# Written-out engine orders, FFN blocks placed among attention, paired output projections: an adaLN block on one Trainium2 core

## The chip, the cores and the metric

The kernel runs on one core of a Trainium2 chip. The metric is the device time of one execution in microseconds; several runs of each kernel are taken, beside runs of the kernel before on the same chip. The profiled run gives a span (first to last instruction), which lies about 2 us under the time of the same run (227.9 under 230.01 before, 216.1 under 217.79 after). Engines: PE is TensorE (PEld its weight loads), DVE VectorE, ACT ScalarE, POOL GpSimd. TensorE writes its results to the banks of a memory called PSUM. The names of these results in the profiles: ps_w warm-up, ps_c and ps_m the six vectors made from c, ps_t a norm's transposes, ps_qk, ps_v, ps_l logits, ps_o values, ps_ot transposes of o, ps_g gates, ps_wo output projection, ps_h and ps_y the two halves of the FFN.

On one core a run is called slow when it is over 1.5% above the fastest of the same kernel. Where I compare kernels I use fast runs, and say so where a trace is of a slow one.

## The reference, cut to what matters

```python
x = A_x                                              # 2048 x 448, bf16
sa, ca, ga, sb, cb, gb = (silu(c) @ w_mod)           # six vectors of 448
h = layernorm(x) * (1 + ca) + sa
x = x + ga * (local_attention(h @ wqkv) @ wo)        # 16 heads of 28; 8 keys per query, every second row
h = layernorm(x) * (1 + cb) + sb
x = x + gb * (silu(h @ w1) @ w2)                     # the FFN, 448 -> 1792 -> 448
```

Rows are split by parity (`par`), so that "every second row" is a run of neighbours. Attention works on 18 blocks: nine of 114 queries (`e0` to `e8` in the new code) for each parity. A block is two groups of logits on TensorE, two exponentials on ScalarE, a mask on VectorE, a values product, a division, a transposition. FFN and both norms work in four chunks of 512 rows.

## The kernel before: the parts that the change touches

The kernel lists about 700 operations with dependencies, durations and buffers, and lets a small scheduler put them into an order. The engines then take their instructions strictly in that order.

```python
class Plan:
    def emit(self, seed, spread, rounds):          # 12 rounds of list scheduling
        ...
        for _ in range(rounds):
            span, new = self.order(prio)
            if span < self.span:
                self.span, got = span, new
            prio = {i: -t + spread * (rnd.random() - 0.5) for i, t in self.late(new or got).items()}
        ...
```

A number of matmuls without use warm TensorE's clock up at the start:

```python
    def warm_up(o):
        ...
        T.matmul(warm[0][:, 0, :], lhsT=ident[:], rhs=ident[:].unsqueeze(1).to_broadcast([128, 4, 128]), start=True, stop=True)
```

The output projection takes one unit (128 rows of one parity) at a time. D is 448, so the last of the four contraction steps has 64 rows:

```python
    def out_proj(k, i, par):
        def wo_mm(o):
            box["ps"] = onet("ps_wo")                          # one of 2 single PSUM banks
            for kk in range(KT):
                T.matmul(box["ps"][:, 0:D], lhsT=oT[rows_of(kk), kk, par, s0:s0 + 128], rhs=wo[rows_of(kk), kk, :], ...)
```

Logits, QK, V, a norm's transposes and FFN1 use three pairs of banks (`big`); values, transposes of o, gates and FFN2 two single ones (`one`). At the end of the program all exponentials are queued ahead of all silus (cut):

```python
    for k in range(NC):
        first = silus.get(k - LA - 1, [sc_op]) + (exps[k - 1][-1:] if k else [])     # LA = 3, NC = 4
        for b in BLOCKS[k]: ... logits(...); values(...)
        if k >= LA: ffn1(k - LA, exps[k])
    for k in range(NC - LA, NC):
        ffn1(k, silus[k - 1]); ffn2(k - 1)
    ffn2(NC - 1)
```

## Time and profile before

| | before |
|---|---|
| time, median of 3 runs | 228.67 us (227.53 to 229.92) |
| span of the profiled run | 227.9 us (its own time was 230.01) |
| TensorE / VectorE / ScalarE busy | 210.9 / 111.6 / 102.9 us |
| TensorE at half clock, by the record | 11.3 to 14.7, 35.15 to 48.8, 103.4 to 120.5 |
| first V matmul; last matmul | 16.0; 222.5 |
| TensorE idle between these two | 9.1 us |

To read it: TensorE is busy 93% of the span, but a busy TensorE at half clock does half the work. So three things are to be had: the time until the projections can start, idle TensorE after that, and half clock after that. The lines behind the table stand in the prediction.

### The profile page before, as it was taken

How to read it: one execution, taken by the hardware profiler on the slowest of the kernel's cores; microseconds unless marked ns; L12 is line 12 of the kernel's file. 1: busy time of each engine (PE TensorE's matmuls, PEld its weight loads, DVE VectorE, ACT ScalarE, POOL GpSimd, SP SyncE). 2: the span in 40 equal slices, each digit the busy share in tenths (PEclk: the TensorE clock that was granted, in tenths of full speed). 3: DMA queues.
4: the chain of work that ended last, by engine and by line, in shares of the span. 5: the costliest groups of instructions: out<-in, count | busy, mean ns of one | idle time of the engine just before them, and what ended most of it. 6: DMA issues, size and time to landing. Idle time of an engine off the chain costs nothing.

```text
span 227.9 us, 3929 instructions
## 1 busy us (share of the span) xinstructions
PE 210.9 (93%) x1656; PEld 99.3 (44%) x1656; DVE 111.6 (49%) x245; ACT 102.9 (45%) x125; POOL 20.2 (9%) x60
## 2 busy tenths in 40 slices
PE   7899997999899999955999899999999999999990
PEld 2643445434444544434544343435444345444450
DVE  3539795691588485798652735664111021102211
ACT  1118766735786785790667253361215503350000
POOL 6303311000002000150000010111000000000000
PEclk9979995579999999995559999999999999999998
DMA  6999900000000000000000000000000001001111
GB/s 225 347 389 334 305 6 1 0 3 0 3 1 3 0 3 0 3 0 0 4 0 3 0 0 3 0 0 0 23 30 30 0 23 40 20 1 42 43 43 47
DMA packets 7856, 11.28 MB, mean 49 GB/s; under 512 B 536, under 2 KB 6616, under 8 KB 7832
## 3 DMA queue, kind: packets, MB, share of 16 engines
q1 hardware_dynamic: 7824, 10.95, 14.5%
q8 instruction: 15, 0.25, 0.5%
q14 instruction: 9, 0.07, 0.1%
q10 hardware_dynamic: 8, 0.00, 0.0%
HBM read 9.12 MB, written 1.84 MB: 48 GB/s over the span
## 4 chain that ended last, share of the span: by engine, by line
PE 80%; DVE 9%; ACT 4%; issue 2%; DMA 1%; ACTq 0%; DVEq 0%
PE ps_y L705 19%; PE ps_h L681 17%; PE ps_qk L513 10%; PE ps_v L536 6%; PE ps_wo L659 5%; PE ps_t L424 4%; PE ps_l L566 3%; PE ps_h L683 3%; PE ps_o L623 3%; PE ps_m L375 3%; PE ps_t L426 2%; ACT p L574 2%; PE ps_ot L636 2%; DVE st L409 2%; ACT h L433 2%
## 5 line engine op out<-in xcount | busy, mean ns | idle before, releaser
L687 ACT ACTIVATE both<-ps_h 128x1024 bf16<-128x1024 f32 x28 | 28.5, 1024 | 47.6 <-PE ps_y L705 21.6
L705 PE MATMUL ps_y<-w,both 128*128 128x448 bf16 x224 | 44.4, 353 | 0.7 <-DVE ot L710 0.7
L681 PE MATMUL ps_h<-h,w 128*128 128x512 bf16 x168 | 41.8, 389 | 0.0
L574 ACT ACTIVATE p<-ps_l 128x912 bf16<-128x912 f32 (+1 forms) x36 | 31.6, 939 | 11.3 <-PE ps_l L566 11.2
L710 DVE TENSOR_TENSOR ot<-ps_y,x_all 128x448 bf16<-128x448 f32 x16 | 9.7, 622 | 54.2 <-PE ps_y L705 54.2
L705 PEld LDWEIGHTS <-both 128*128 128x128 bf16 x224 | 21.4, 98 | 21.7 <-issue 2.1
L513 PE MATMUL ps_qk<-h,wp 128*128 128x512 bf16 (+1 forms) x128 | 28.9, 399 | 0.0
L681 PEld LDWEIGHTS <-w 128*128 128x128 bf16 x168 | 15.2, 99 | 19.8 <-issue 4.6
L433 ACT ACTIVATE h<-ps_t,modc 128x512 bf16<-128x512 bf16 x18 | 13.0, 776 | 18.3 <-DVE h L435 13.3
L409 DVE BATCH_NORM_STATS2 st<-x_all 128x6 f32<-128x448 bf16 x32 | 19.7, 615 | 3.2 <-DMA x_all<-in_A_x_dram 2.8
L596 DVE TENSOR_TENSOR p<-p,maskb 128x1824 bf16<-128x1824 bf16 (+1 forms) x18 | 19.3, 1094 | 2.4 <-ACT p L574 2.4
L517 ACT CAST qk<-ps_qk 128x1024 bf16<-128x1024 f32 x14 | 14.2, 1013 | 11.6 <-PE ps_qk L513 11.6
L413 POOL TENSOR_TENSOR rs<-mv,epsb 128x2 f32<-128x2 f32 x16 | 4.8, 300 | 133.3 <-DVE mv L410 133.3
L659 PE MATMUL ps_wo<-wo,oT 128*128 128x448 bf16 x64 | 16.4, 356 | 0.0
L513 PEld LDWEIGHTS <-wp 128*128 128x128 bf16 (+1 forms) x128 | 9.3, 98 | 15.7 <-issue 8.1
L536 PE MATMUL ps_v<-wqkv,h 128*128 128x448 bf16 (+1 forms) x72 | 15.9, 379 | 0.1
L566 PE MATMUL ps_l<-qk 28*128 28x114 bf16 (+1 forms) x288 | 13.4, 229 | 2.7 <-ACT p L574 1.7
L662 DVE TENSOR_TENSOR x_all<-ps_wo,x_all 128x448 bf16<-128x448 f32 x16 | 9.9, 617 | 11.0 <-PE ps_wo L659 10.9
L418 DVE TENSOR_SCALAR xn<-x_all,mv,rs 128x448 bf16<-128x448 bf16 x32 | 11.4, 389 | 5.2 <-POOL rs L414 3.5
L424 PE MATMUL ps_t<-ident,xn 128*128 128x128 bf16 x96 | 12.7, 252 | 0.1
L414 POOL TENSOR_TENSOR rs<-rs,negh 128x2 f32<-128x2 f32 x16 | 12.0, 751 | 1.3
L566 PEld LDWEIGHTS <-qk 28*128 28x128 bf16 x288 | 8.2, 101 | 8.1 <-issue 6.4
(77 smaller groups left out, 172.4 us busy)
## 6 DMA issues: line engine op xcount, KB each, us to landing
x_all<-in_A_x_dram SPq DMA_DIRECT2D x4, 448.0 KB, 5.2
out_dram<-ot SPq DMA_DIRECT2D x16, 112.0 KB, 1.7
w<-in_B_w_dram SPq DMA_DIRECT2D x1, 1568.0 KB
both<-in_w_mod_dram SPq DMA_DIRECT2D x1, 1344.0 KB, 11.2
w<-in_B_w_dram SPq DMA_DIRECT2D x1, 1344.0 KB, 14.4
wqkv<-in_A_wqkv_dram SPq DMA_DIRECT2D x1, 1008.0 KB, 7.2
both<-in_w_mod_dram SPq DMA_DIRECT2D x1, 672.0 KB, 5.2
wo<-in_A_wo_dram SPq DMA_DIRECT2D x1, 336.0 KB, 11.1
```

Of the source, the lines that this page charges most:

```text
L409: V.bn_stats(out=st[:], in_=x_all[:, us[j], :])
L424: T.transpose(box["ps"][:, k, 128 * j:128 * j + 128], box[j][:, 128 * k:128 * k + 128], ident[:])
L433: S.activation(out=out_, in_=in_, func=ACTF.Identity, scale=scale, bias=shift)
L513: T.matmul(ps[:, j, :], lhsT=w.rearrange("p h d -> p (h d)"), rhs=h[rows_of(kk, j), kk, :, 128:128 + CP], start=start, stop=stop)
L536: T.matmul(ps[:, par, 0:D], lhsT=h[rows_of(kk, par), kk, par, b0:b0 + 128], rhs=w, start=(kk == 0), stop=(kk == KT - 1))
L566: T.matmul(ps[:, j, g * nq:(g + 1) * nq], lhsT=key, rhs=q, start=True, stop=True)
L574: S.activation(out=out_, in_=ps[:, :, 0:4 * nq].rearrange("p j (g q) -> p j g q", q=nq), func=ACTF.Exp, scale=SCALE)
L596: V.tensor_tensor(out=p, in0=p, in1=maskb[:, 1 if b == 0 else 0, 0:nq].unsqueeze(1).to_broadcast([128, H, nq]), op=ALU.mult)
L659: T.matmul(box["ps"][:, 0:D], lhsT=oT[rows_of(kk), kk, par, s0:s0 + 128], rhs=wo[rows_of(kk), kk, :], start=(kk == 0), stop=(kk == KT - 1))
L681: T.matmul(ps[:, j, :], lhsT=w1[:, kk, c0:c0 + 128], rhs=h[:, kk, :], start=start, stop=stop)
L687: return [(("act", act_ns(1024)), lambda o, ps: S.activation(out=hid[:, k % 2, :, i, :], in_=ps[:], func=ACTF.Silu), after + f2_read.get(k ...
L705: T.matmul(box["ps"][:, 0:D], lhsT=hid[:, k % 2, f % 2, f // 2, 128 * j:128 * j + 128], rhs=w2[:, f // 2 + 7 * (f % 2), :], start=(f == 0) ...
```

## The change

Its intent: replace 12 rounds of scheduling in the program by an order found offline, by a search that models TensorE's clock; let FFN blocks alternate with attention; use the array's two halves in the output projection; let the first norm's four units go one by one. For the projection, the last 64 rows of wo are loaded twice, into both halves (cut below). The diff, cut to its core:

```diff
-WARM = 26
-LA = 3
-SEED, SPREAD, ROUNDS = 0, 2000.0, 12
+WARM, WARM_AT = 22, 1500.0
+SEQ = "e0 e1 e2 e3 e4 s0 e5 e6 s1 e7 e8 s2 s3"
+ORDER = (
+    "42 0 3 2 1 22 23 4 24 25 66 26 32 5 79 40 43 41 30 36 31 44 37 76 34 45 38 80 ..."   # 707 entries, cut
+)
...
+    S.preload_act_table(ACTF.Silu)
+    V.memset(junk[:], 0.0)
     V.memset(c4[:], 0.0)
...
-        T.matmul(warm[0][:, 0, :], lhsT=ident[:], rhs=ident[:].unsqueeze(1).to_broadcast([128, 4, 128]), start=True, stop=True)
+        T.matmul(warm[0][:, 0, :], lhsT=junk[:, 0:128], rhs=junk[:], start=True, stop=True)
...
-            for j in (0, 2):                                  # norm: rstd for two units at once
+            for j in range(0, 4, n):                          # n = 1 for the first norm, else 2
...
-            box["ps"] = onet("ps_wo")
-            for kk in range(KT):
-                T.matmul(box["ps"][:, 0:D], lhsT=oT[rows_of(kk), kk, par, s0:s0 + 128], rhs=wo[rows_of(kk), kk, :], ...)
+            ps = box["ps"] = bigt("ps_wo")
+            for kk in range(KT):
+                for par in range(2):
+                    T.matmul(ps[:, par, 0:D], lhsT=oT[rows_of(kk, par), kk, par, s0:s0 + 128], rhs=wo[rows_of(kk, par), kk, :], ...)
...
+    for kind, n in ((x[0], int(x[1:])) for x in SEQ.split()):
+        if kind == "e": ...                                   # attention block n
+        else:
+            ffn1(n, e_last + s_last, l_last)
+            s_last, f_last = silus[n], f1_read[n]
+            ffn2(n)
...
-    P.emit(SEED, SPREAD, 1 if safe else ROUNDS)
+    P.emit("" if safe else ORDER)
```

## The prediction

> **What bounds the kernel now.** I read the page first, then the windows, then the chain of work that ended last, then TensorE's waits. The page:
>
> ```profile
> span 227.9 us, 3929 instructions
> PE 210.9 (93%) x1656; PEld 99.3 (44%) x1656; DVE 111.6 (49%) x245; ACT 102.9 (45%) x125; POOL 20.2 (9%) x60
> ...
> PE   7899997999899999955999899999999999999990
> ...
> DVE  3539795691588485798652735664111021102211
> ACT  1118766735786785790667253361215503350000
> ...
> PEclk9979995579999999995559999999999999999998
> ```
>
> TensorE (PE) is busy 93% of the span, no other engine half of it. So TensorE's time is the bound, but not all of that time is work: the clock row has two holes, slices 7 and 8 and again 20 to 22, in which the same matmuls take up to twice as long. And VectorE and ScalarE are busy in the first 23 slices, almost free in the last 17: attention stands first, the feed-forward part (FFN) last. Windows cut at a step of 3.413 us show the holes' edges exactly (columns: window, its length, busy times, PEclk):
>
> ```profile
> 31.74:35.15 3.41, 3.41 (x47) 2.17 (x45) 3.38 (x9) 2.75 (x3) 0.78 (x2) 1.00 0.02 5
> 35.15:38.56 3.41, 2.42 (x44) 2.09 (x45) 1.48 (x6) 1.26 (x2) 0.11 (x1) 0.50 0.01 2
> ...
> 100.00:103.42 3.42, 0.47 (x14) 0.27 (x10) 3.39 (x6) 2.50 (x4) 2.40 (x2) 1.00 0.00 0
> 103.42:106.83 3.41, 1.88 (x31) 1.33 (x32) 2.98 (x9) 0.00 (x0) 0.00 (x0) 0.50 0.00 0
> ```
>
> The clock is half in 11.3 to 14.7, 35.15 to 48.8 and 103.4 to 120.5: 34 us. In the window before each fall the array streamed little: the 40 one-column matmuls of ps_m, or an idle PE. The last fall has this wait ahead of it:
>
> ```profile
> PE ps_ot L636 <- DVE o L630: 4.4, 1, 4.4
> PE ps_l L566 <- ACT p L574: 1.7, 4, 1.0
> ```
>
> Between 16.0 (first V matmul) and 130 PE is busy 105.54 of 114.00 us, idle 8.5; from 130 to 222.3 it is idle 0.7, at full clock. The tail from the last matmul to the end is 5.6 us. So what can be won lies before 130: idle time, half clock, and the start.
>
> **The Trainium skill.** "TensorE: Matmul & The Clock Gate", What's actually happening, says that a monitor sets the clock to half or full by how busy the array was in a free-running window of 3413 ns. The trace agrees: all six edges lie on one grid of 3.413 us (35.15 to 48.8 is 4 steps, 103.4 to 120.5 is 5). It gives no threshold. I took one from this trace: columns streamed in a window, at the granted clock, over what the array could stream. The windows that ended in a fall held 0.13, 0.34 and 0.02; the poorest warm ones that did not, 0.42 and 0.44. Cold windows at 0.75 and below stayed cold; those that ended in a rise held 0.82 and more. "TensorEngine Tiling (Array Packing)", Key Properties, says that changing the tiling mode drains TensorE. The trace shows this at the 64-row step of each projection group: weight loads wait 0.37 and 0.20 us for "issue" around it. "ScalarE: Activation LUTs", What ACT_TABLE_LOAD costs, gives about 1283 ns and a drain of 1380 ns; here the load is 1283 ns, and the exponential that follows starts 0.02 us after it, so I use 1.28.
>
> **The work on TensorE.** From the chain, where pieces follow each other without a wait at full clock:
>
> ```profile
> 63.23 1.93 PE ps_wo L659 x8
> 65.16 0.31 PE ps_l L566 x8
> 65.47 1.54 PE ps_v L536 x8
> 67.00 0.31 PE ps_l L566 x8
> ...
> 68.85 0.49 PE ps_o L623 x16
> ...
> 211.75 10.39 PE ps_y L705 x54
> ```
>
> Read so: ps_y 0.192 us a matmul; V 1.53 a block; logits 0.31 a group; values 0.50; in the same way ps_h 3.13 for 16, QK 3.25 for 16, a norm's transposes 0.45 a unit, ps_ot 0.43, ps_g 0.97, ps_m 2.86. The list: ps_y 224 x 0.192 = 43.0, ps_h 43.8, QK 26.0, V 9 x 1.53 = 13.8, output projection 16 x 0.965 = 15.4, transposes 32 x 0.45 = 14.4, logits 36 x 0.31 = 11.2, values 9.0, ps_ot 7.7, ps_m 5.7, gates 1.9. Without the warm-up and what lies before 16.0 (one ps_m, four transposes) 187.4 us is left. Measured from 16.0 to 222.3: 206.3. The excess of 18.9 is 9.1 idle, some 8 to 9 of half clock, and 1.5 to 2 at the boundaries between kinds.
>
> **The change, part by part.**
> *Output projection in pairs.* Sixteen groups of four matmuls become eight groups of eight, in which the two 64-row steps lie on the two halves of the array, as V has them. From 1.93 to 1.53 for two units: 0.4 x 8 = 3.2 us of TensorE time. The trace has PE as the chain there, so I count it whole. Work after the start: 184.2.
> *Order: FFN into attention.* The order of the instructions shows two of the four FFN blocks within attention. Before, at the last pair of logits groups, PE's list had 90 us behind it and DVE's 84, by durations of the trace: the two engines were bound together, and each waited for the other. After, it is 129 against 94. From the ninth pair on (PE's list at about 66 us) every stretch between two pairs has more PE work than ACT or DVE work. I cut PE's new list into pieces of 3.413 us and took their activity: from 70 us on none is under 0.69, so no fall there. The hole at 103 to 120 and its 5 us wait should go: about 9 us. The wait at 126 to 129 too (1.5 us).
> *Table loads.* Exponential and silu alternate: seven loads in place of three, 4 x 1.28 = 5.1 us on ACT, which goes from 103 to 108 of some 216. Off the path, except where PE waits for a fresh table with all three PSUM pairs full.
> *The start.* The silu table is loaded ahead of everything, but on the queue that also issues the load of c (at 1.02 before). That issue moves to about 2.3, c lands near 6.0 in place of 4.74, and sc follows at once: before, sc began at 6.11. Nothing won there. The warm-up no longer needs the identity (1.43 to about 1.1), but has 6 matmuls ahead of c in place of 11, then a gap of over 2 us and 8 more, perhaps cold, which hold ps_m back. The four transposes follow ps_m at once instead of five warm-up matmuls (1.7 us). I take V's start at 15.0 (13.5 to 16.5) for 16.0.
> *First norm.* Four single rstd steps for two double ones: xn was done at 9.3 and the transposes began at 12.25, so it was not on the path; 0 us.
> *Not won: 15 to 45 us.* PE's new order has seven logits groups in a row there. Their seven exponentials take 7 x 0.94 = 6.6 us, the PE work is 2.2 us, and three PSUM pairs let PE run only three ahead: about 3 us idle. My walk through the lists puts the end of these groups at 41.6, before it was 40.4; the new order has one V block more behind it by then. So the first 40 us win nothing but what the start wins. In that idle window the activity is near 0.15, so the clock falls, and comes back in the QK matmuls after it: 2.5 to 3 us. The second ps_m stands among QK matmuls (piece at 0.26, fall if the grid lies badly): 1.2 us on average.
>
> The sum: start 15.0 + work 184.2 + boundaries 1.7 + tail 5.6 = 206.5; losses 3 (first exponentials) + 2.8 (cold after them) + 1.2 (ps_m) + 1.5 (DVE-tied stretch 45 to 70, still as much DVE as PE work) + 0.7 (the two waits for ps_y's banks at the end, which stay) = 9.2. Span 215.7. The time before lies 0.8 over its span: 216.5.
>
> **Rivals.** (1) DVE stays the bound of attention: its work, 111.6 us, is unchanged. For it: to the eighth pair the lists are level, 59.8 PE to 56.5 DVE. Against: FFN blocks lie between after that. If right, 4 to 6 us of idle and one more cold hole: 222 to 224. (2) The waits turn into PSUM waits: the pairs of the projection now take from the three pairs of banks that logits, QK and FFN1 use. For it: FFN1 and QK want two of three at once. Against: two banks of the other kind are freed. If right, 2 to 3 us: 219. (3) The search's order is nearly free of waits on the chip as well: losses of 4 only, 211.
>
> **Range and chances.** The low end is rival 3, 211; the high end rival 1 with a poor start, 222. Within 2% would need over 224, which leaves less than half of the 12 us of idle, cold and pairing won. Faster by over 2%: 0.92; within 2%: 0.07; slower: 0.01.
>
> **What would show it.** Mean clock rising from 0.92 to 0.95 or more with no half-clock window after 70 us, but one near 38 to 45; eight ps_wo runs of 1.53; seven table loads; the first V matmul near 15; PE's last matmul 5.6 us before the end; PE idle from the first V to that under 7 us. It is wrong if the clock falls again after 70 us, if PE waits longest for DVE o or x_all in the middle, or if the first V starts after 17.

## The result, and the profile after

The changed kernel took 217.87 us (median of 4 runs, 216.87 to 219.79), the kernel before 229.09 us beside it. The ratio of the fast runs is 0.953 (95% interval 0.944 to 0.961). Ratios are the mean time of one kernel's fast runs over that of the other's of the same rounds, so not quite the ratio of the medians. The predicted 216.5 us (211 to 222) holds, and the span, 216.1, lies 0.4 from the predicted 215.7. The next lines show that this is partly luck.

The page of the changed kernel, its total line of busy times and three rows of slices:

```profile
PE 201.6 (93%) x1652; PEld 96.3 (45%) x1652; DVE 111.8 (52%) x246; ACT 107.3 (50%) x127; POOL 21.6 (10%) x65
...
DVE  3608934798679886255361620898518441102220
ACT  2006538784487487744755966860453243550000
...
PEclk9999999988999999999999999999999999999998
```

The long hole of the middle is gone: past slice 10 the clock row has no dip. From 130 us to the last matmul VectorE is now busy 33.4 of 80.4 us and ScalarE 31.7; before it was 24.2 and 27.3 of 92.3. The waits of TensorE after the first V (engine, line, what it waited for: us in total, times, longest):

```profile
PE ps_l L569 <- ACT p L577: 1.2, 3, 0.4
PE ps_o L626 <- DVE p L599: 1.1, 1, 1.1
PE ps_l L569 <- DVE h L438: 0.9, 1, 0.9
PE ps_f L774 <- DVE cnt L772: 0.8, 1, 0.8
PE ps_wo L663 <- ACT p L577: 0.3, 1, 0.3
```

The 4.4 us wait for o has no successor. The first three lie between 41 and 47, where the predicted wait for the first exponentials is. Only 1.2 of their 3.2 us end on an exponential; the other 2.0 end on VectorE, which does 2.2 us of gate products for w2 at 43.64 to 45.86 and the mask after them. With these waits comes the one half-clock window that the record shows (window, length, busy times, clock):

```profile
43.34:46.76 3.42, 1.33 (x32) 0.67 (x25) 3.42 (x7) 3.42 (x5) 0.00 (x0) 1.00 0.00 0
46.76:50.17 3.41, 3.23 (x24) 1.29 (x26) 3.38 (x8) 1.12 (x2) 0.00 (x0) 0.50 0.00 0
50.17:53.58 3.41, 3.41 (x35) 1.65 (x32) 3.29 (x5) 2.18 (x3) 0.00 (x0) 1.00 0.02 5
```

TensorE is busy 1.33 of 3.42 us, the clock falls, and 10 QK matmuls take 3.15 us instead of the 2.03 that follow from 3.25 for 16: a loss of 1.1 us.

**What the record hides: the start.** The timeline of PE in the changed kernel (start, duration, ...; what ended the idle time before, in brackets):

```profile
1.26 2.74 PE L349 MATMUL ps_w<-junk 128*128 128x512 bf16 x6 [1.26 <-DVE scT L270]
6.99 0.18 PE L361 MATMUL ps_c<-ident,sc 4*128 4x4 bf16 x1 [2.99 <-ACT sc L356]
7.10 3.60 PE L349 MATMUL ps_w<-junk 128*128 128x512 bf16 x8
10.49 3.36 PE L378 MATMUL ps_m<-scT,both 128*128 128x1 bf16 x40
...
16.50 3.56 PE L349 MATMUL ps_w<-junk 128*128 128x512 bf16 x9
```

Eight warm-up matmuls in 3.6 us are 0.43 us each, twice the 0.217 from start to start of the last two of the nine below. So the clock is at half, although PEclk reads 9 there: in all fourteen traces the record opens with a fall and shows full clock before it, and here the first recorded fall is at 46.8. The durations give the true state. Of the nine warm-up matmuls that begin at 16.50 some seven are slow and the last ones fast: the clock rose at about 19.5. That is on the same grid of 3.413 us as 46.76, 8 steps earlier. The first V matmul runs at 19.90; I had predicted 15.0, and the kernel before had it at 16.0.

So the 11.8 us by which the span fell are made of five terms (both traces are of fast runs, that of the kernel before the slower end of them: 230.01 us beside a median of 228.67):

| term, us | before | after | difference |
|---|---|---|---|
| start to first V | 16.0 | 19.9 | +3.9 |
| work after it (list of the prediction) | 187.4 | 184.2 | -3.2 |
| idle after it | 9.1 | 4.6 | -4.5 |
| half clock and boundaries after it (what is left over) | 10.0 | 1.7 | -8.3 |
| last matmul to end | 5.4 | 5.7 | +0.3 |

### The profile page after: what moved, and what is told of

Read it like the earlier page. It is cut to its first block, busy times and chain, and to the rows that moved or that the text cites. A ratio compares the mean times of both kernels' runs of the same rounds, so it can differ in the third digit from the quotient of the medians.

```text
span 216.1 us, 3926 instructions
## 1 busy us (share of the span) xinstructions
PE 201.6 (93%) x1652; PEld 96.3 (45%) x1652; DVE 111.8 (52%) x246; ACT 107.3 (50%) x127; POOL 21.6 (10%) x65
## 4 chain that ended last, share of the span: by engine, by line
PE 88%; DVE 4%; ACT 2%; DMA 2%; issue 1%; ACTq 0%
PE ps_y L711 20%; PE ps_h L687 18%; PE ps_qk L516 13%; PE ps_v L539 6%; PE ps_wo L663 5%; PE ps_t L427 4%; PE ps_o L626 4%; PE ps_h L689 4%; PE ps_l L569 3%; PE ps_w L349 3%; PE ps_m L378 3%; PE ps_t L429 3%; DMA c<-in_c_dram 2%; PE ps_ot L639 1%; PE ps_ot L641 1%; DVE w L739 1%
## 5 line engine op out<-in xcount | busy, mean ns | idle before, releaser
L711 PE MATMUL ps_y<-w,both 128*128 128x448 bf16 x224 | 45.8, 353 | 0.0
L687 PE MATMUL ps_h<-h,w 128*128 128x512 bf16 x168 | 40.8, 380 | 0.0
L520 ACT CAST qk<-ps_qk 128x1024 bf16<-128x1024 f32 x14 | 14.1, 1013 | 16.5 <-PE ps_qk L516 16.5
L416 POOL TENSOR_TENSOR rs<-mv,epsb 128x2 f32<-128x2 f32 (+1 forms) x18 | 6.1, 337 | 151.2 <-DVE mv L413 151.2
L412 DVE BATCH_NORM_STATS2 st<-x_all 128x6 f32<-128x448 bf16 x32 | 19.5, 609 | 2.6 <-DMA x_all<-in_A_x_dram 2.4
L599 DVE TENSOR_TENSOR p<-p,maskb 128x1824 bf16<-128x1824 bf16 (+1 forms) x18 | 19.5, 1094 | 2.4 <-ACT p L577 2.3
L436 ACT ACTIVATE h<-ps_t,modc 128x512 bf16<-128x512 bf16 x14 | 10.1, 774 | 20.7 <-DVE h L438 18.4
L438 DVE TENSOR_SCALAR h<-ps_t,modc 128x512 bf16<-128x512 bf16 x18 | 8.9, 539 | 13.9 <-ACT h L436 8.3
L539 PE MATMUL ps_v<-wqkv,h 128*128 128x448 bf16 (+1 forms) x72 | 14.3, 355 | 0.0
L569 PE MATMUL ps_l<-qk 28*128 28x114 bf16 (+1 forms) x288 | 11.7, 210 | 2.3 <-ACT p L577 1.2
L663 PE MATMUL ps_wo<-wo,oT 128*128 128x448 bf16 (+1 forms) x64 | 12.8, 354 | 0.3 <-ACT p L577 0.3
L417 POOL TENSOR_TENSOR rs<-rs,negh 128x2 f32<-128x2 f32 (+1 forms) x18 | 12.1, 670 | 1.4
L631 DVE RECIPROCAL rc<-ps_o 114x16 f32<-114x16 f32 (+1 forms) x18 | 4.5, 252 | 14.4 <-PE ps_o L626 14.2
```

Of the source, the lines that this page charges most:

```text
L412: V.bn_stats(out=st[:], in_=x_all[:, us[j], :])
L417: G.tensor_tensor(out=rs[:, j:j + n], in0=rs[:, j:j + n], in1=negh[:, 0:n], op=ALU.pow)
L520: return [(either(act_ns(1024), dve_ns(1024)), lambda o, ps: copy_on(o)(out=qk[:, :, g, :, s0:s0 + CP], in_=ps[:].rearrange("p j (t s) -> ...
L539: T.matmul(ps[:, par, 0:D], lhsT=h[rows_of(kk, par), kk, par, b0:b0 + 128], rhs=w, start=(kk == 0), stop=(kk == KT - 1))
L569: T.matmul(ps[:, j, g * nq:(g + 1) * nq], lhsT=key, rhs=q, start=True, stop=True)
L599: V.tensor_tensor(out=p, in0=p, in1=maskb[:, 1 if b == 0 else 0, 0:nq].unsqueeze(1).to_broadcast([128, H, nq]), op=ALU.mult)
```

## The experiments

My theories were these. A: the pairing saves drains on the path; the start is late because the warm-up stops too early; the alternation fills the waits. B: what pays in the order is that its search knew the clock. C, against B: what pays is a long search, and an order without waits has full windows anyway. D, after the first results: alternation and search are both needed.

All twelve runs gave correct results. "After start" is the time from the first V or QK matmul to the last matmul; idle is TensorE's within it; half clock is what the record shows within it. These four come from the one trace of each run. The medians are of all runs; where some were slow, the fast ones stand beside them.

| run | median us (range of the fast runs) | start | after start | idle | half clock |
|---|---|---|---|---|---|
| before | 228.67 | 16.0 | 206.5 | 9.1 | 30.7 |
| changed kernel | 217.87 (216.9 to 219.8) | 19.9 | 190.5 | 4.6 | 3.4 |
| the same once more | 215.80 (214.8 to 216.9) | 17.9 | 190.5 | 4.6 | 3.4 |
| pairing undone | 219.26 (218.3 to 220.2) | 17.7 | 194.3 | 4.2 | 6.8 |
| 13 warm-ups ahead of c | 217.48 (fast: 213.5, 214.3) | 15.2 | 190.6 | 4.6 | 3.4 |
| 10 ahead, table load later | 215.21 (fast: 213.9 to 216.0) | 16.0 | 190.3 | 4.6 | 3.4 |
| short search, alternating | 225.60 (fast: 220.9) | 14.6 | 204.9 | 5.8 | 37 (slow run) |
| short search, attention first | 227.64 (227.4 to 228.5) | 14.8 | 207.1 | 9.9 | 33 |
| long blind search, alternating | 213.36 (212.6 to 213.9) | 15.7 | 189.9 | 1.9 | 11 |
| long search with clock, alternating | 217.29 (215.4 to 218.0) | 16.0 | 195.0 | 4.4 | 12 |
| long blind search, attention first | 218.84 (217.9 to 220.6) | 15.3 | 195.9 | 3.5 | 20 |
| long blind search, warm-ups moved | 212.89 (211.9 to 213.4) | 16.8 | 188.7 | 1.8 | 10 |

### Pairing undone

```diff
-            for kk in range(KT):
-                for par in range(2):
-                    T.matmul(ps[:, par, 0:D], lhsT=oT[rows_of(kk, par), ...], rhs=wo[rows_of(kk, par), kk, :], ...)
+            for par in range(2):
+                for kk in range(KT):
+                    T.matmul(ps[:, par, 0:D], lhsT=oT[rows_of(kk), ...], rhs=wo[rows_of(kk), kk, :], ...)
```

> The changed kernel with the output projection issued as before: inside each of the eight operations the two units follow each other, four matmuls each, both 64-row steps on the same half. Same order of everything else. Theory A (pairing saves drains on a chain that TensorE bounds): eight ps_wo groups of about 1.93 us in place of 1.43 to 1.59, so +2.5 to +3.2 us, a span near 219. Rival (the saved time falls into waits): less than +1 us.

The chain of the changed kernel, then that of this run, at the same two groups:

```profile
63.08 1.59 PE ps_wo L663 x8
73.18 1.44 PE ps_wo L663 x8
```

```profile
61.93 1.99 PE ps_wo L663 x8
72.43 1.84 PE ps_wo L663 x8
```

It is 0.40 us a group, 0.39 in the median of the seven groups in the chains, so 3.1 us of TensorE's work for eight: the predicted 3.2. But the eighth group (at 162 to 164) gains nothing on the path: the wait for cnt, the program's check of its sums, follows it, and is 0.8 us in the changed kernel and 0.4 here:

```profile
PE ps_f L774 <- DVE cnt L772: 0.4, 1, 0.4
```

So the path gains 2.7 us. The part after the start grew by 3.8 us; the 1.1 left over may go with a second half-clock window that this trace has. Nor is all of the 0.39 a drain (TensorE running empty at a change between full height and 64 rows). By the single records of the trace, a matmul of 448 columns follows the one before it by 0.189 us, the change to 64 rows takes 0.285 and the change back 0.292. The pair saves one such turn of 0.19, since the two 64-row matmuls start within 3 ns of each other, and 0.20 for one change there and back. The median rose by only 1.4 us against the first runs of the changed kernel and by 3.5 against the second, which shows how much the start blurs: the start in this trace is 17.7 where that of the changed kernel was 19.9, with nothing changed there. Theory A holds for the pairing in the trace, with half of the saving from drains; the rival (under +1 us) falls.

### The start

Thirteen warm-up matmuls ahead of ps_c (entries 48 to 54 of the order moved ahead of 67):

```diff
-    "... 39 67 29 48 81 7 28 49 82 68 50 51 77 52 83 78 53 54 86 55 69 70 ..."
+    "... 39 48 49 50 51 52 53 54 67 29 81 7 28 82 68 77 83 78 86 55 69 70 ..."
```

> The changed kernel with seven of the warm-up matmuls moved from behind ps_c to ahead of it: 13 before c and 1 after, in place of 6 and 8; same 23 in all. Theory A (the 6 matmuls leave a 3 us gap, no window of 3.4 us is full enough, and the clock stays half until 19.5): the warm-up runs without a gap to about 6.8, the clock rises by 8, ps_m starts near 7.5 in place of 10.7, the first V near 14 to 16.5 in place of 19.9, so -3.5 to -5.5 us. Rival (the start is set by the arrival of c and of the weights, the clock is incidental): V within 1 us of 19.9, time the same.

The timeline of PE in this run:

```profile
1.26 4.61 PE L348 MATMUL ps_w<-junk 128*128 128x512 bf16 x13 [1.26 <-DVE scT L269]
6.28 0.17 PE L360 MATMUL ps_c<-ident,sc 4*128 4x4 bf16 x1 [0.41 <-POOL v L337]
6.38 0.39 PE L348 MATMUL ps_w<-junk 128*128 128x512 bf16 x1
6.70 0.21 PE L377 MATMUL ps_m<-scT,both 128*128 128x1 bf16 x3
```

Thirteen in 4.61 us: the first ones slow, the rest fast, so the clock rose before 6. ps_m begins at 6.70 instead of 10.49, the first V at 15.2 instead of 19.9, and the part after it takes 190.6 us, as before. In the trace theory A is right to its number, against the first trace of the changed kernel. Against its second trace (below, first V at 17.9) the gain is 2.7 us, and this run does not tell the clock from the place: there the eight warm-up matmuls between ps_c and ps_m take 3.4 us, and would take 1.7 at full clock; here a single one stands between. In the times it is only half right: two runs at 213.5 and 214.3, two slow ones at 220.7 and 220.9, with a recorded mean clock of 0.936 against 0.975 and more.

> A second look at the version with 13 warm-up matmuls ahead of c. Its four runs were 213.5, 214.3, 220.7 and 220.9. As above: near 213 with some 7 us at half clock, near 220 if the trace shows another long half-clock stretch, and then the place of it.

214.88 us: start 16.2, half clock at 8.3 to 15.1 and for 6.8 us at 42 to 49. What the slow runs do stays open.

Next, the table load moved behind the issue of c, with ten warm-ups ahead:

```diff
-    S.preload_act_table(ACTF.Silu)
...
-    ld_c.append(P.op(("none", 3200.0), none))
+    ld_c.append(P.op(("none", 3200.0), lambda o: S.preload_act_table(ACTF.Silu)))
```

> As the run before it, but the silu table is loaded after the issue of c's load instead of ahead of it, and 10 warm-up matmuls stand before ps_c, 4 after. Theory A: c lands near 4.8 in place of 6.55, sc begins near 4.9; ps_m is then held by the modulation weights, which land near 6.5 to 7, so it starts near 7; the first V another 0.5 us earlier than with 13 matmuls alone, if the clock rises as early. -4 to -6 us against the changed kernel. Rival (table load and issue order do not matter): the same as with 13 matmuls alone.

> A second look at the version with the table load behind the issue of c and 10 warm-up matmuls ahead of it. If the spread of its four runs (213.9 to 220.9) comes from where the clock's windows fall, this trace shows other edges than the first (fall at 8.6, rise at 15, one more stretch at 42 to 45.6), and the time goes with the length of the half-clock stretches: near 213 with 10 us of them, near 220 with 25.

Here the rival wins. The issue of c stands at 1.29 with the load ahead of it or behind it, and sc began at 5.89 and 6.54 in the two looks, against 6.62 and 5.82 in the two of the changed kernel. My sentence "that issue moves to about 2.3" was wrong: the table load runs from 0.81 to 2.09 in the changed kernel, and the issue behind it goes out at 1.29 all the same. c simply lands later here than in the kernel before (4.69 us after its second issue in the first trace, against 3.18), while 0.3 us later in issue; I have not found out why. The two looks took 214.4 and 215.2 us with the first V at 16.0 and 17.8; the spread between them lies in the start, as expected, but neither look was a 220. (The first trace's edges, by its record, are 8.2, 15.1, 42.4 and 45.8; the expectation has them up to 0.4 off.)

The changed kernel once more:

> The changed kernel once more, beside the two searched orders on the same chip. Expected by every theory: 216 to 220 us. Theory A of the start: if the clock rises before 19 us in this trace, because the windows lie otherwise, the first V comes earlier than 19.9 by about that much.

First V at 17.9, 2.0 us earlier than in the first trace, and the same 190.5 us after it, to 0.1. The span is 1.6 us shorter. So in these two traces of one order the part after the start repeats, and the start is what varies. The PE timeline shows how:

```profile
6.30 3.60 PE L349 MATMUL ps_w<-junk 128*128 128x512 bf16 x8
9.69 2.96 PE L378 MATMUL ps_m<-scT,both 128*128 128x1 bf16 x40
12.58 0.34 PE L427 MATMUL ps_t<-ident,xn 128*128 128x128 bf16 x3
14.61 3.47 PE L349 MATMUL ps_w<-junk 128*128 128x512 bf16 x9
17.91 2.27 PE L539 MATMUL ps_v<-wqkv,h 128*128 128x448 bf16 x11
```

Here the same eight warm-up matmuls did raise the clock: ps_m takes 2.96 us instead of 3.36, three transposes 0.34 instead of 0.50. The grid of this trace has an edge at 10.56 (the recorded fall at 44.69 less 10 steps), just behind them; in the first trace an edge at 9.23 cut them in two. After ps_m the clock fell again (13.97 to 17.38 by the record), so the nine warm-up matmuls ahead of V are slow here too. The run with the pairing undone, which has the same start, shows the same with V at 17.7.

### What in the order pays

The changed kernel's operations, ordered by the old scheduler (12 rounds), first alternating, then with attention ahead of FFN:

```diff
-ORDER = ( ... )
+SEED, SPREAD, ROUNDS = 0, 2000.0, 12            # late() and emit() of the kernel before put back
```

```diff
-SEQ = "e0 e1 e2 e3 e4 s0 e5 e6 s1 e7 e8 s2 s3"
+SEQ = "e0 e1 e2 e3 e4 e5 e6 e7 e8 s0 s1 s2 s3"
```

> The changed kernel without its written order: the old scheduler of the kernel before (12 rounds of random priorities, no clock model) orders the same operations, FFN blocks still alternating with attention. Theory A (letting FFN into attention is what fills the waits): no half-clock window after 70 us, TensorE idle between 70 us and its end under 3 us; 215 to 220 us. Rival (the long offline search is what pays): 222 us or more, with new waits for ACT or DVE in the middle.

> As the run with the old scheduler on the changed kernel's operations, but all of attention ahead of all FFN blocks, as in the kernel before. Theory A (the alternation fills waits): TensorE idle between the first V and its last matmul 8 to 10 us again (5.8 with alternation), a half-clock stretch of over 10 us before the first FFN block, 225 to 229 us. Rival (alternation does little by itself, only the written order pays): within 1% of the run with alternation, 221 to 226 us.

With attention first the paired kernel takes 227.6 us, a ratio of 0.999 (0.991 to 1.007) to the kernel before: pairing and the rest of the change give nothing there, the old scheduler loses them in waits and half clock. With alternation it takes 220.9 in its one fast run and 224.8 to 226.6 in three slow ones. TensorE's idle time falls as theory A said, 9.9 to 5.8 us; but the alternating trace (a slow run, so not to be compared with the fast ones) has half clock again from 136 to 146, which theory A excluded. Its fast run's mean clock of 0.938 still stands for some 27 us at half clock (2 x 0.062 x 218.8). So alternation is not enough; the order matters, and idle time is not the measure of it.

That made theory B look good, and I tested it with a search of my own: the same operations and dependencies, with PE durations corrected from the traces, and some 92,000 to 100,000 rounds of random changes of priority. Once its score was blind to the clock, once it counted the clock with thresholds near those of the prediction (fall under 0.40, rise over 0.80).

```diff
-ORDER = ( ... )
+ORDER = ( ... )                                 # order of the blind search / of the search with the clock
```

> The changed kernel's operations with an order of my own: 100,000 rounds of a search over the same dependencies and durations that knows nothing of the clock. Theory B (what pays is that the search knows the clock; the old scheduler with alternation left TensorE idle only 5.8 us but at half clock for 39 us): half-clock stretches over 20 us again after the first V, 221 us or more. Rival C (what pays is the length of the search: an order without waits has full windows by itself): under 12 us at half clock after the first V, 213 to 218 us.

> As the run before it, but the search scores each order with the clock: it falls after a window of 3.413 us with under 0.40 of the columns streamed, and rises after one with over 0.80, averaged over eight positions of the windows. Theory B: at least 3 us faster than the order of the clock-blind search. Rival C: within 1.5 us of it.

Theory B falls. The blind order takes 213.4 us and beats the changed kernel on the same chip (215.8); the order with the clock takes 217.3. Both have about 11 to 12 us of half clock after the start; the blind one waits 1.9 us, the other 4.4. These are single orders of a random search, so they do not rank the two scores, nor do they show what a better model of the clock would bring. They do show that an order can be had without any knowledge of the clock that is as good as the written one and better.

The last question: would length alone have done, without alternation?

> All of attention ahead of the FFN blocks, ordered by the same clock-blind search of the same length (92,000 rounds) as the order that took 213.4 us with the blocks alternating. Rival C (the search's length alone pays): within 2 us of 213.4. Theory D (both are needed: without FFN matmuls among them, attention's matmuls stream too few columns, and the clock falls even where TensorE does not wait): TensorE idle under 6 us after its first QK, but 20 us or more at half clock, 217 to 224 us.

The clock rows of the two long blind searches, first alternating, then attention first:

```profile
PEclk9976996699999999999999999999999999999999
```

```profile
PEclk9958995599999999967999999999999999999999
```

With attention first it is 218.8 us, 5.5 more, and 5.9 more than the version of the next section. It waits only 1.6 us more than the alternating one (3.5 against 1.9) but has 20 us of half clock instead of 11, with two more windows at 93 to 97 and 100 to 104, in attention, where its TensorE is idle 3.2 us out of 60. Theory D holds as far as one order of each kind can show it. With attention first the search brings 8.8 us (227.6 to 218.8), with alternation 7.5 (220.9, one fast run, to 213.4); alternation brings 6.8 us with the old scheduler and 5.5 with the long search. Whether the search's length pays, or its corrected durations, was not tested apart.

### A version that beats both

The warm-ups of the blind order dealt out otherwise (13 ahead of c, 2 behind it, 8 between the first transposes and the first QK):

> The order of the long clock-blind search with its 23 warm-up matmuls dealt out otherwise: 13 ahead of ps_c, 2 behind it, 8 between the first transposes and the first QK, where TensorE waits 2 us in that order and the clock is at half. Theory A (the start pays for a cold clock): first QK 0.5 to 1.5 us earlier and at full clock, -1 to -2.5 us, about 211.5. Rival: the warm-up matmuls themselves hold the QK back, within 0.7 us of 213.4.

The time is 212.9 us against 213.4, so the rival holds: within 0.7 us. They were run at other times. The blind order, then this one, at the first QK:

```profile
15.69 3.93 PE L515 MATMUL ps_qk<-h,wp 128*128 128x512 bf16 x10 [1.97 <-ACT h L435]
```

```profile
16.84 2.10 PE L515 MATMUL ps_qk<-h,wp 128*128 128x512 bf16 x10
```

The first QK comes at 16.8 instead of 15.7, but at full clock all but its first 0.2 us; the next half-clock stretch is one window longer (30.7 to 40.9 for 33.4 to 40.3). In sum the start is 1.1 us longer and the rest 1.2 shorter. The blind order beats the changed kernel by 1.1% (213.36 for 215.80), this version beats it by 1.3 to 2.3%, and both beat the kernel before by 6.5% (ratio 0.935, 0.928 to 0.942 for this one).

## Why the prediction was right or wrong, point by point

The total is right, and so is the class of reasons: the gain lies ahead of 130 us, in idle time, half clock and pairing, and the FFN blocks close the hole at 103 to 120. Two terms of the sum were wrong by nearly the same amount in opposite directions.

| term of the sum, us | predicted | measured |
|---|---|---|
| start to first V | 15.0 (13.5 to 16.5) | 19.9 (17.9 in the second trace) |
| work | 184.2 | same list; pairing 3.1 for 3.2 |
| boundaries | 1.7 | 0.6, what is left over |
| first exponentials | 3 | 3.2 (1.2 + 1.1 + 0.9) |
| half clock after them | 2.8 | 1.1 |
| half clock from the second ps_m | 1.2 | 0, no fall |
| DVE-tied stretch 45 to 70 | 1.5 | 0.3 |
| waits for ps_y's banks | 0.7 | 0; instead 0.8 for cnt |
| last matmul to end | 5.6 | 5.7 |

- **The step that failed** is "I take V's start at 15.0 (13.5 to 16.5) for 16.0". I had seen that six warm-ups leave a gap and that the eight after it would "perhaps" be cold and hold ps_m back, but gave this no size, and did not count the nine ahead of V at all. The starts in the timelines give the sizes:

  | stretch of the start, us | before | after | difference | second trace, difference |
  |---|---|---|---|---|
  | to ps_c | 6.47 | 6.99 | +0.52 | -0.29 |
  | ps_c to ps_m (warm-up matmuls between: 6 warm before, 8 cold after) | 1.41 | 3.50 | +2.09 | +2.10 |
  | ps_m to the transposes (5 warm-up matmuls before, none after; I had 1.7) | 4.37 | 3.29 | -1.08 | -1.48 |
  | transposes | 2.67 | 2.72 | +0.05 | -0.64 |
  | last warm-up matmuls to the first V (5 before, 9 cold after) | 1.09 | 3.40 | +2.31 | +2.21 |

  So both traces hold 2.1 and 2.2 to 2.3 us of warm-up matmuls that I had not counted; they differ in when c came and in the clock after ps_m's start. V could have begun before the nine were through: the first parts of h that it reads were done at 17.62,

```profile
16.62 1.00 DVE L438 TENSOR_SCALAR h<-ps_t,modc 128x512 bf16<-128x512 bf16 x2 [2.31 <-PE ps_t L429]
```

  2.3 us ahead of V, while in the kernel before V began at 16.01 with these parts done at 16.03; wqkv had landed by 11.0. It would have begun at half clock; what leaving the nine out brings was not tested in this order, and in the blind order eight such matmuls cost what they gave. In the first trace the clock did not come back before 19.5. On the grid through 19.47 the windows were these:

```profile
2.41:5.82 3.41, 1.59 (x4) 0.30 (x2) 1.67 (x5) 0.00 (x0) 2.32 (x15) 1.00 1.02 343
5.82:9.23 3.41, 2.24 (x7) 0.85 (x8) 2.53 (x8) 0.47 (x2) 2.77 (x13) 1.00 1.01 349
9.23:12.65 3.42, 3.42 (x32) 2.41 (x30) 0.40 (x1) 0.00 (x0) 0.04 (x1) 1.00 1.05 335
...
16.06:19.47 3.41, 3.41 (x13) 1.17 (x11) 2.82 (x7) 1.76 (x3) 0.00 (x0) 1.00 1.06 289
```

  Only the last is full of dense matmuls; the two before it (the one left out, 12.65 to 16.06, reads much as the one shown) are busy all the time, but with ps_m's one-column matmuls and transposes. My own threshold (0.82 and more to rise) could have warned me, had I laid the windows over the new start as I did over the part after 70 us; the second trace, with the rise near 10.6, shows that it depends on where the grid lies. The prediction's own sign, "wrong if the first V starts after 17", came true; the sum was saved by the other terms.
- **The losses after the start** were 9.2 and boundaries 1.7; together 6.3 was measured. The wait for the first exponentials was right in size, but by luck: I had counted exponentials and PSUM pairs alone, and 2.0 of the 3.2 us ended on VectorE. The fall after it cost one window, not two; the second ps_m was cut in two by an edge of the grid at 29.7, so neither window was poor enough; I had given that a weight, and it was the good case.
- **The first 40 us win nothing but what the start wins**: right. The end of the seven logits groups came at 45.8, predicted 41.6, the difference being the later start.
- **Pairing**: right for the work (3.1 for 3.2), measured by itself; counting it whole was not, since one of the eight savings fell into the wait for cnt (2.7 on the path).
- **FFN into attention**: right that no window fell after 70 us with this order. That the alternation does this by itself was not so: with the old scheduler it left half clock at 136 to 146 in the slow run that was traced, and 220.9 us in the fast one. Nor is it the only thing that closes the hole at 103 to 120: the long search with attention first leaves 6.8 us of half clock there (93 to 97, 100 to 104).
- **Table loads**: seven, as predicted, and ScalarE at 107.3 of the predicted 108. What they cost by themselves was not tested.
- **First norm**: 0 us fits, as its last xn was done by 9.7 and the transposes began at 13.8; not tested by itself.
- **Rivals**: the middle was nearest to rival 3 (losses of 4); waits that end on VectorE (1) are 2.8 us in all and waits that end on an exponential 1.5, by the lines shown; which of them are waits for a PSUM pair (2), the lines do not say.
- **Readings of the prediction to put right**: the second hole of the clock row is slices 19 to 21. ScalarE was not almost free in the last slices (27.3 of the 92.3 us from 130 on). The list's terms as printed leave 187.2, not 187.4, by rounding. And the 0.8 us from span to time set a median of 228.67 against the span of a run that took 230.01; with the 2.1 us of that run itself, the time would have been 217.8.

## What to carry to other kernels

Lay the clock's windows over the start of a program too, and read the clock there from the durations of equal matmuls, not from a clock record that begins with its first fall. Whether a warm-up works depends on where the windows lie: the same eight matmuls raised the clock in one trace and not in the other, and thin work after them (ps_m) let it fall again. A warm-up matmul on the path also costs its own time, twice as much while the clock is at half: 2.1 and 2.3 us more than before here. Mixing a dense stage into a thin one helps TensorE twice, by filling waits and by keeping windows full, but the order decides how much: a longer blind search over the same operations was worth 7.5 to 8.8 us here, the mixing 5.5 to 6.8 (single orders, one of them with one fast run), and in the one order tried a model of the clock brought nothing.

## What the Trainium skill lacked or had wrong

- "TensorE: Matmul & The Clock Gate", What's actually happening: the window of 3413 ns agrees with every edge measured here, but no threshold is given. In the trace of the kernel before, windows with 0.34 of the columns streamed ended in a fall and 0.42 did not; 0.75 did not end in a rise and 0.82 did, as I count them. A busy TensorE is not enough: the window from 7.85 to 11.26 there is busy for 3.41 of 3.41 us, mostly with ps_m's one-column matmuls, and ended in a fall.
- The same section puts the ramp at under 1% of a typical kernel span. Here the first V of the same start moved between 17.7 and 19.9 us from run to run, and to 15.2 with the warm-up rearranged: 4.7 us, 2.2% of the span. The ramp is only a part of that, but not one to leave out of a sum. (That the ramp varies from run to run, the section says too.)
- The same page, Part 4: PE-mode transpose, says that the full clock does not engage for transposes. Here three of them take 0.27 us to the next start at full clock (12.58 to 12.85 in the second trace of the changed kernel) and 0.43 at half (13.78 to 14.21 in the first), so they do run faster once the clock is up. The trace does not say whether they run in the mode that the page means, nor whether they count as busy.
- "ScalarE: Activation LUTs", What ACT_TABLE_LOAD costs, adds a drain of 1380 ns to a load of 1283 ns. In the changed kernel the work before the load ends at 36.04, the load of 1.28 us begins at 36.05 and its exponential at 37.34: no drain is to be seen.
- On no page that I read: what a change of tiling mode costs. Here it is 0.10 us into a 64-row step (0.285 for 0.189 from start to start) and 0.10 out of it (0.292).
